# A spectral-filter and feed-forward block on one core: first-layer weights in four quarters, twelve tiles transposed by the DMA crossbar, smaller token blocks

## The chip, the cores and the metric

The kernel runs on one core of a Trainium2 chip. The metric is the device time of one execution in microseconds (us). Each comparison was made on one chip in alternating rounds of the changed kernel and the kernel before. An execution's state is *slow* when it is over 1.5% above the fastest of its kernel; comparisons use the others, the *fast* ones. The median given with an experiment is over all its executions, the ratio over the fast ones alone. A profile is one execution.

## The reference

The input x has 2048 tokens of 640 features in bf16. Its layer norm goes two ways: through a two-dimensional FFT, a product with a complex filter and the inverse FFT, and through a feed-forward layer with 1536 hidden units. Both results are added to x.

```python
xn = layernorm(x)                                   # over the 640 features
a  = irfft2(rfft2(xn) * (w_r + 1j * w_i))           # filter of 2048 x 321
b  = gelu(xn @ w1 + b1) @ w2 + b2                   # 640 -> 1536 -> 640
out = x + a + b
```

## The kernel before

The FFTs are matrix products with small tables. The stages, by the names that the profile shows: `gtab` (first FFT step, along tokens), `etab` (along features), `mtab` (second token step, out of the copy `Xb`), the filter product on DVE (`T<-Y,Wf`), `ntab`, `getab` and `htab` (the inverse). Among these stand the matmuls of the first layer, `xnT,W`, and of the second, `W,gT`. They are TensorE's filler: whenever an FFT step waits for a copy, they run.

The profile calls TensorE PE (its weight loads PEld), VectorE DVE, ScalarE ACT, GpSimd POOL and SyncE SP. L12 is line 12 of the kernel.

All operations go to a list scheduler in the kernel itself, which simulates the engines with rough durations and fixes the order on each engine and in the DMA queue by priorities (`PRIO`). PSUM banks are dealt out from zones (`ZONE`). So a changed priority or block size can change the whole order.

Sixteen tiles of 128 tokens are normalized by DVE. The first layer needs them with the features on the partitions, `xnT`. The first eight are transposed on TensorE through PSUM, the others by the crossbar in the DMA:

```python
if c < BYPE:                                   # BYPE = 8
    ...                                        # five transposes on TensorE, then a copy on DVE or ACT
else:
    ring_ops.append(K.op([("sp", 1.25)], 50, lambda e, _, c=c, xnv=xnv: e.dma_start(
        xnT[:, :, 128 * c:128 * c + 128], xnv(0, [[1, D]]), transpose=True), ...))
```

The filter `Wf` is loaded by eight large loads (rows as they lie, pieces of 10,272 bytes) and ten for the mirrored rows. These have to be read in reverse order, so they go in pieces of one row, 642 bytes; the eight longest have 240 or 256 such pieces each. A load may start only after the load four places earlier has landed (`DEPTH = 4`). The first filter product waits for all of them:

```python
for j, row, n in ((0, 128 - m1, 16),) if m1 else ((0, 64, 1), (1, 127, 15)):
    load_w(<rows j..j+n of Wf>, <rows of w_r or w_i, step -321>, ...)      # mirrored
...
K.op([("dve", ...)], pr, <T = Y * Wf>, reads=[Y, B_w, B_wpad], writes=[TB], after=ring_ops)
```

Every one of these loads, and every transpose by DMA, is issued by SyncE into one queue and served by the same 16 DMA engines.

## Time and profile before

| | before |
|---|---|
| median of 3 runs | 159.98 us (158.77 to 160.95) |
| span of the profiled execution | 155.0 us, clock 1.00 |
| TensorE busy | 147.4 us, 95% |
| DVE busy | 124.4 us, 80% |
| transposes by DMA | 8, median 5.8 us from issue to landing |

Three more readings matter for what came. The first is the DMA's busy share in the first 60 us in 40 slices of 1.5 us, one digit each (9 is 90% or more):

```profile
DMA  0769999999999733993799999999999988000000
```

The 16 DMA engines have slack between 19.5 and 30 us (but for two full slices), then work without a gap until 51 us. The second is DVE's timeline at the first filter product (start, length, what):

```profile
51.15 1.57 DVE L713 TENSOR_TENSOR T<-Y,Wf 128x1288 bf16<-128x1288 bf16 x2
```

No bracket follows the line, so DVE did not wait ahead of it: the filter was there. In the DMA's records, the last mirrored piece ended at 47.1 us, and its load was reported as landed at 47.6. The margin was about 3.5 us. The third is the busy time of the engines from 50 to 60 us (PE, PEld, DVE, ACT, POOL, then granted clock, DMA share and GB/s):

```profile
50.00:60.00 10.00, 9.84 (x120) 4.90 (x115) 8.93 (x17) 7.03 (x13) 0.00 (x0) 1.00 0.08 20
```

### The profile page before, as it was taken

The numbers are of one execution on the slowest core, as the hardware profiler recorded it, in microseconds if no ns is written. First come the engines' busy times: TensorE is split into PE (matmuls) and PEld (weight loads), VectorE is DVE, ScalarE is ACT, GpSimd is POOL, SyncE is SP. The second block draws the span as 40 slices with busy tenths as digits, with TensorE's granted clock in tenths as the row PEclk, the third lists the DMA queues.
The fourth block names the chain that finished last, engine by engine and source line by source line (L and its number), as shares of the span: only waits on it lengthen the run. The fifth ranks groups of instructions, "written<-read, shape, count | busy, mean of one in ns | idle before, by whom it ended". The sixth has DMA issues, their size and how long they took to land.

```text
span 155.0 us, 3617 instructions
## 1 busy us (share of the span) xinstructions
PE 147.4 (95%) x1473; PEld 95.5 (62%) x1483; DVE 124.4 (80%) x277; ACT 73.1 (47%) x144; POOL 30.3 (20%) x33
## 2 busy tenths in 40 slices
PE   5699999999999999999999999999999999999993
PEld 2298996545564545454555666777776667777771
DVE  3869999999964989898898797899999989822231
ACT  3077987888776678868767534310101330000000
POOL 1201121110100000000000003009937254444100
PEclk9999999999999999999999999999999999999999
DMA  4999949799999000019141400002533442211111
GB/s 116 346 377 395 329 110 172 98 138 146 101 134 225 18 4 0 4 16 324 25 149 18 156 0 12 34 0 89 169 105 127 123 132 84 73 42 42 63 66 44
DMA packets 18632, 17.85 MB, mean 115 GB/s; under 512 B 6712, under 2 KB 17336, under 8 KB 18488
## 3 DMA queue, kind: packets, MB, share of 16 engines
q1 hardware_dynamic: 18448, 17.59, 47.5%
q8 instruction: 11, 0.18, 0.5%
q10 hardware_dynamic: 168, 0.04, 0.1%
q14 instruction: 5, 0.04, 0.1%
HBM read 13.69 MB, written 2.62 MB: 105 GB/s over the span
## 4 chain that ended last, share of the span: by engine, by line
PE 74%; DVE 14%; DMA 4%; issue 3%; ACT 2%; SPq 1%
PE ps L477 73%; DVE Wf L806 4%; DMA W<-in_B_w_dram 4%; DVE Wf L811 4%; DVE ost L836 3%; DVE Wf L487 2%; ACT gT L657 2%; PE ps L602 1%; DVE xnT L792 1%; SPq L472 1%; ACT xnT L484 0%; ACT b1col L558 0%
## 5 line engine op out<-in xcount | busy, mean ns | idle before, releaser
L477 PE MATMUL ps<-xnT,W 128*128 128x512 bf16 (+2 forms) x350 | 56.6, 306 | 2.7 <-DMA W<-in_B_w_dram 1.3
L477 PE MATMUL ps<-W,gT 128*128 128x320 bf16 x384 | 56.7, 299 | 0.0
L477 PEld LDWEIGHTS ps<-W,gT 128*128 128x128 bf16 x384 | 37.0, 98 | 14.2 <-issue 0.3
L477 PEld LDWEIGHTS ps<-xnT,W 128*128 128x128 bf16 x360 | 28.5, 98 | 19.7 <-issue 1.8
L657 ACT ACTIVATE gT<-ps,b1col 128x512 bf16<-128x512 f32 (+2 forms) x72 | 36.5, 550 | 5.0 <-PE ps L477 4.7
L823 POOL TENSOR_TENSOR xo<-xr,b2bc 128x640 f32<-128x640 bf16 x11 | 16.4, 1494 | 20.9 <-DVE ost L836 20.9
L836 DVE TENSOR_TENSOR ost<-ps,xo 128x640 bf16<-128x640 f32 (+1 forms) x12 | 9.2, 764 | 13.6 <-PE ps L477 13.6
L823 POOL TENSOR_TENSOR xnT<-xr,xnT 128x640 f32<-128x640 bf16 x5 | 7.4, 1490 | 60.3 <-DVE Zs L487 55.0
L484 ACT ACTIVATE Wf<-ps 128x640 bf16<-128x640 f32 x9 | 6.2, 704 | 25.9 <-PE ps L477 25.9
L574 DVE BATCH_NORM_STATS2 stats<-XV 128x6 f32<-128x320 bf16 x32 | 14.3, 474 | 2.3 <-DMA XV<-in_A_x_dram 2.3
L713 DVE TENSOR_TENSOR T<-Y,Wf 128x1288 bf16<-128x1288 bf16 x16 | 12.7, 828 | 0.6
L582 POOL TENSOR_TENSOR rstd<-ve,mhalf 128x2 f32<-128x2 f32 (+1 forms) x9 | 6.2, 693 | 32.1 <-DVE ve L581 32.1
L811 DVE TENSOR_TENSOR Wf<-Wf 128x640 bf16<-128x640 bf16 x16 | 11.8, 775 | 0.1
L806 DVE TENSOR_TENSOR Wf<-Wf 128x640 bf16<-128x640 bf16 x16 | 10.4, 682 | 0.1
L487 DVE CAST Y<-ps 128x644 bf16<-128x644 f32 x8 | 6.6, 828 | 4.4 <-PE ps L477 4.4
L484 ACT ACTIVATE Xb<-ps 128x640 bf16<-128x640 f32 x8 | 7.1, 890 | 4.3 <-PE ps L477 4.3
L477 PE MATMUL ps<-getab,XV 128*128 128x160 bf16 (+1 forms) x128 | 8.6, 233 | 0.4 <-DVE ost L836 0.2
L484 ACT ACTIVATE XW<-ps 128x640 bf16<-128x640 f32 x12 | 8.3, 704 | 1.3 <-PE ps L477 1.1
L484 ACT ACTIVATE XV<-ps 128x640 bf16<-128x640 f32 x9 | 6.2, 703 | 5.6 <-PE ps L477 5.6
L477 PE MATMUL ps<-etab,XW 128*128 128x160 bf16 (+1 forms) x128 | 8.6, 233 | 0.0
L487 DVE CAST Xb<-ps 128x640 bf16<-128x640 f32 x8 | 7.1, 883 | 1.2 <-PE ps L477 1.2
L477 PEld LDWEIGHTS ps<-etab,XW 128*128 128x128 bf16 (+1 forms) x128 | 5.4, 95 | 4.2 <-ACT Xb L484 0.4
(48 smaller groups left out, 140.9 us busy)
## 6 DMA issues: line engine op xcount, KB each, us to landing
W<-in_B_w_dram SPq DMA_DIRECT2D x6, 640.0 KB, 5.5
xr<-in_A_x_dram SPq DMA_DIRECT2D x16, 160.0 KB, 2.3
out_dram<-ost SPq DMA_DIRECT2D x15, 160.0 KB, 1.8
XV<-in_A_x_dram SPq DMA_DIRECT2D x7, 320.0 KB, 9.3
Wf<-in_A_w_r_dram SPq DMA_DIRECT2D x7, 160.5 KB, 10.2
Wf<-in_A_w_i_dram SPq DMA_DIRECT2D x7, 160.5 KB, 5.4
gtab<-c_G SPq DMA_DIRECT2D x1, 512.0 KB, 8.8
htab<-c_H SPq DMA_DIRECT2D x1, 512.0 KB, 3.7
```

What stands on the lines that cost most here:

```text
L472: return K.op([(eng, 0.45)], 0, lambda e, _: e.dma_start(dst, src), reads=reads, writes=[buf], after=after, nbytes=nbytes, rate=rate)
L477: ins = e.matmul(o_, lhsT=lw, rhs=rh, start=st, stop=sp_)
L484: return e.activation(dst(), src(), ACT.Copy, scale=scale)
L487: return e.tensor_copy(dst(), src())
L574: K.op([("dve", 0.4)], 100 - c, lambda e, _, c=c, h=h: e.bn_stats(stats[:, c, 6 * h:6 * h + 6], view(XV, c * D + H2 * h, [[1, H2]])), read ...
L582: K.op([("pool", 0.75)], 100 - c, lambda e, _, a=a, b=b: e.tensor_tensor(out=rstd[:, a:b], in0=ve[:, a:b], in1=mhalf[:, 0:b - a], op=ALU.pow),
L657: K.op([("act", act_us(s1 - s0, 1))], pr + PRIO["gelu"], lambda e, _, s0=s0, s1=s1, fc=fc, hps=hps: e.activation(gT[:, fc, s0:s1], ps(hps. ...
L713: t_ops[pair].append(K.op([("dve", dve_us(4 * KP, 2))], pr, lambda e, _, k=k, Y=Y, TB=TB, pair=pair: e.tensor_tensor(out=view(TT, TB.slot ...
L806: K.op([("dve", dve_us(D, 2))], pr + 2, lambda e, _, k=k, op=op, yo=yo, y2=y2: e.tensor_tensor(out=view(Wf, Y2 + y2.slot * 2 * D + (H2 - 1 ...
L811: K.op([("dve", dve_us(D, 2))], pr + 3, lambda e, _, k=k, op=op, y2=y2, yf=yf: e.tensor_tensor(out=view(Wf, YF + yf.slot * 2 * D + (D - 1) ...
L823: K.op([("pool", pool_us(640))], 50, lambda e, _, c=c, xr=xr, xov=xov: e.tensor_tensor(out=xov(0, D), in0=halves(xrt[:, xr.slot, :]), in1= ...
L836: os_ops.append(K.op([("dve", dve_us(H2 * len(hs)))], 95, lambda e, _, a=a, b=b, hs=hs, xov=xov, fps=fps, os_=os_: e.tensor_tensor(out=hal ...
```

## The change

The change wants TensorE to start earlier and to do less. First-layer weights come in quarters, so that less has to land before the first matmul; twelve tiles instead of eight are transposed by DMA, which takes 20 transposes and four copies off the engines; token blocks are smaller, so that a block can start with fewer tiles. To give the early transposes room, four table loads and one filter load are held back until four transposes have been issued. The other constants (zones, priorities, `AHEAD`, `STAGED`) came with it from a new tuning.

```diff
-ZONE = {'hps': ((0, 8), (4, 8), (4, 8), (0, 4), (6, 8), (6, 8)), 'bps': (0, 6), ...
-PRIO = {'hps': 37.4, ... 'eps': 59.4, 'fin': 18.3, 'fst': 17.7}
-BLOCKS = ((0, 1), (1, 2), (2, 4), (4, 8), (8, 12), (12, 16))
-AHEAD = 3
-STAGED = (0, 2, 4, 7, 9)
+ZONE = {'hps': ((2, 8), (0, 8), (4, 8), (4, 8), (4, 8), (4, 8), (4, 8)), 'bps': (0, 4), ...
+PRIO = {'hps': 61.1, ... 'eps': 12.2, 'fin': 1, 'fst': 14.5}
+BLOCKS = ((0, 1), (1, 2), (2, 4), (4, 6), (6, 9), (9, 12), (12, 16))
+AHEAD = 2
+STAGED = (0, 2, 4, 6, 8)
-BYPE = 8
+BYDMA = (4, 5, 6, 7, 8, 9, 10, 11, 12, 13, 14, 15)
 ...                                                   (durations in the scheduler's model: cut)
-        W1 = sb("W1", [128, 3, 5, 512])
+        W1 = sb("W1", [128, 4, 5, 384])
 ...
         load_w1(0)
         load_w1(1)
+        load_w1(2)
         load_x(2, 2)
-        load_w1(2)
+        load_w1(3)
 ...
-        load(etab[:], ...)  load(mtab ...)  load(ntab ...)  load(getab[:], ...)
+        later = [load(etab[:], ...), load(mtab ...), load(ntab ...), load(getab[:], ...)]
 ...
-            if c < BYPE:
+            if c not in BYDMA:
 ...
+        for o in later + few[0:1]:
+            o.gate += [p for p in ring_ops if p.nbytes][:max(0, len(BYDMA) - 8)]
```

(`W2` is loaded in quarters too. Each list of loads is cut to one line here.)

More of the change, by code (lines that the diff above doesn't have):

```diff
@@ L112, in pool_us @@
     return 0.075 + n / 500.0
-ZONE = {'hps': ((0, 8), (4, 8), (4, 8), (0, 4), (6, 8), (6, 8)), 'bps': (0, 6), 'cps': (0, 6), 'dps': (0, 6), 'eps': (0, 4), 'fps': (2, 8), 'fst': (0, 8), 'yps': (0, 4), 'tps': (0, 2), 'aps': (2, 6)}
-PRIO = {'hps': 37.4, 'gelu': 82.7, 'pb': 120.8, 'pc': 154.1, 'filt': 90.5, 'ipc': 148.4, 'xb': 65.5, 'eps': 59.4, 'fin': 18.3, 'fst': 17.7}
-BLOCKS = ((0, 1), (1, 2), (2, 4), (4, 8), (8, 12), (12, 16))
-AHEAD = 3
-STAGED = (0, 2, 4, 7, 9)
+ZONE = {'hps': ((2, 8), (0, 8), (4, 8), (4, 8), (4, 8), (4, 8), (4, 8)), 'bps': (0, 4), 'cps': (0, 8), 'dps': (0, 4), 'eps': (0, 4), 'fps': (4, 8), 'fst': (4, 8), 'yps': (0, 8), 'tps': (0, 4), 'aps': (0, 6)}
+PRIO = {'hps': 61.1, 'gelu': 149.5, 'pb': 91.9, 'pc': 99.5, 'filt': 154.7, 'ipc': 263.2, 'xb': 214.9, 'eps': 12.2, 'fin': 1, 'fst': 14.5}
+BLOCKS = ((0, 1), (1, 2), (2, 4), (4, 6), (6, 9), (9, 12), (12, 16))
+AHEAD = 2
+STAGED = (0, 2, 4, 6, 8)
 XRAT = 4
@@ L180 @@
 BIAS = {"dve": 0.0}
+FAST = 7
 LAT = {"pe": 0.2, "dve": 0.12, "act": 0.15, "pool": 0.1}
@@ L211, in schedule @@
     def schedule(self):
-        free = {e: 0.0 for e in self.engines}
+        free = {e: 0.75 for e in self.engines}
         dma_free = port_free = 0.0
@@ L281, in schedule @@
             if o.nbytes:
-                s = max(t + 1.3, dma_free)
+                s = max(t + 1.2, dma_free)
                 dma_free = s + o.nbytes / o.rate
-                o.end = dma_free + 1.7
+                o.end = dma_free + (1.8 if o.seq > FAST else 0.6)
             else:
@@ L499, in bass_parallel_sum__spectral_gfnet__dense_activation_gelu__prompt_kernel @@
         B_x = [Buf(f"x{c}") for c in range(16)]
-        B_w1s = [Buf(f"w1_{j}") for j in range(3)]
+        B_w1s = [Buf(f"w1_{j}") for j in range(4)]
         B_g, B_e, B_m, B_n, B_ge, B_h = [Buf(x) for x in "gemnih"]
@@ L509, in load_w1 @@
         def load_w1(j):
-            load(W1[:, j, :, :], w1v[:, :, 512 * j:512 * j + 512], B_w1s[j], 655360)
+            load(W1[:, j, :, :], w1v[:, :, 384 * j:384 * j + 384], B_w1s[j], 491520, rate=340e3)
         load_x(0, 1)
@@ L522, in bass_parallel_sum__spectral_gfnet__dense_activation_gelu__prompt_kernel @@
             load_x(a, 2)
-        load(etab[:], const["E"], B_e, 204800)
-        load(mtab[:].rearrange("p a b c d -> p (a b c d)"), const["M"], B_m, 131072)
-        load(ntab[:].rearrange("p a b c -> p (a b c)"), const["N"], B_n, 98304)
-        load(getab[:], const["GE"], B_ge, 204800)
         few = []
+        later = [load(etab[:], const["E"], B_e, 204800), load(mtab[:].rearrange("p a b c d -> p (a b c d)"), const["M"], B_m, 131072),
+                 load(ntab[:].rearrange("p a b c -> p (a b c)"), const["N"], B_n, 98304), load(getab[:], const["GE"], B_ge, 204800)]
         def load_w(dst, src, nbytes, rate):
@@ L653, in bass_parallel_sum__spectral_gfnet__dense_activation_gelu__prompt_kernel @@
                     part = [K.op([("pe", len(js) * mm_us(s1 - s0))], pr + 0.01 * len(part), mms(lambda s0=s0, s1=s1, fc=fc, hps=hps, js=js: [
-                        (ps(hps.slot, 0, s1 - s0), W1[:, fc // 4, j, 128 * (fc % 4):128 * (fc % 4) + 128], xnT[:, j, s0:s1], j == 0, j == 4) for j in js]),
-                        reads=[B_w1s[fc // 4]] + B_xnT[c0:c1], writes=[hps], gate=part)]
+                        (ps(hps.slot, 0, s1 - s0), W1[:, fc // 3, j, 128 * (fc % 3):128 * (fc % 3) + 128], xnT[:, j, s0:s1], j == 0, j == 4) for j in js]),
+                        reads=[B_w1s[fc // 3]] + B_xnT[c0:c1], writes=[hps], gate=part)]
                 hps_ops.setdefault(blk, []).append(part[0])
@@ L677, in two @@
             return PS[buf.slot // 2][:, :].rearrange("p (b n) -> p b n", b=2)[:, :, 0:2 * Q4].rearrange("p b (n k) -> p n b k", n=2)
-        IPC = 24 * 0.028 + 0.2
-        FIVE = 8 * mm_us(Q4) + 2 * 0.1 + 0.19
+        IPC = 0.78
+        FIVE = 1.0
         pb_ops, filt_ops, cps_ops, t_ops = [], [], {}, {}
@@ L692, in bass_parallel_sum__spectral_gfnet__dense_activation_gelu__prompt_kernel @@
             cps = [Buf(f"cps{pair}_{r}", psum, 2, ZONE["cps"]) for r in range(2)]
-            cps_ops[pair] = [K.op([("pe", 4 * mm_us(KP) + 0.36)], PRIO["pc"] - pair / 5, mms(lambda pair=pair, cps=cps, xb=xb: [
+            cps_ops[pair] = [K.op([("pe", 0.78)], PRIO["pc"] - pair / 5, mms(lambda pair=pair, cps=cps, xb=xb: [
                 (ps(cps[r].slot + hi, 0, KP)[64 * qq:64 * qq + 64], mtab[64 * hi:64 * hi + 64, 1 if pair == qq == 0 else 0, v, r, :],
@@ L712, in bass_parallel_sum__spectral_gfnet__dense_activation_gelu__prompt_kernel @@
             for k in range(2):
-                t_ops[pair].append(K.op([("dve", dve_us(4 * KP, 2))], pr, lambda e, _, k=k, Y=Y, TB=TB, pair=pair: e.tensor_tensor(
+                t_ops[pair].append(K.op([("dve", 0.05 + dve_us(4 * KP, 2))], pr, lambda e, _, k=k, Y=Y, TB=TB, pair=pair: e.tensor_tensor(
                     out=view(TT, TB.slot * 8 * KP + k * 4 * KP, [[2 * KP, 2], [KP, 2], [1, KP]]), in0=yv(Y, k == 1), in1=wv(pair, k), op=ALU.mult),
@@ L761, in bass_parallel_sum__spectral_gfnet__dense_activation_gelu__prompt_kernel @@
                      reads=[dps[hi]], writes=[B_v[2 * pair + hi]], after=norm_ops)
-        B_w2s = [Buf(f"w2_{i}") for i in range(3)]
-        for i in range(3):
-            load(W2[:, 4 * i:4 * i + 4, :], w2v[:, 4 * i:4 * i + 4, :], B_w2s[i], 655360, after=[o for blk in hps_ops for o in hps_ops[blk][4 * i:4 * i + 4]])
+        B_w2s = [Buf(f"w2_{i}") for i in range(4)]
+        for i in range(4):
+            load(W2[:, 3 * i:3 * i + 3, :], w2v[:, 3 * i:3 * i + 3, :], B_w2s[i], 491520, after=[o for blk in hps_ops for o in hps_ops[blk][3 * i:3 * i + 3]])
         all_hps = [o for blk in hps_ops for o in hps_ops[blk]]
@@ L783, in second @@
                     for fc in range(f0, f0 + 2) for h in hs]),
-                    reads=[B_w2s[f0 // 4]] + [B_gT[block_of[c], fc] for fc in range(f0, f0 + 2)], writes=[fps], gate=part)]
+                    reads=B_w2s[f0 // 3:(f0 + 1) // 3 + 1] + [B_gT[block_of[c], fc] for fc in range(f0, f0 + 2)], writes=[fps], gate=part)]
             return part
```

## The prediction

> **What bounds the kernel now.** I first read the busy shares and the slices on the page. The columns of the first line are busy time, share of the span and instructions; the second has one digit per fortieth of the span (3.9 us).
>
> ```profile
> span 155.0 us, 3617 instructions
> ...
> PE 147.4 (95%) x1473; PEld 95.5 (62%) x1483; DVE 124.4 (80%) x277; ACT 73.1 (47%) x144; POOL 30.3 (20%) x33
> ...
> PE   5699999999999999999999999999999999999993
> ...
> PEclk9999999999999999999999999999999999999999
> ```
>
> TensorE is busy at full clock in every slice but the first two and the last. So the time can change only through the work on TensorE, its idle time at the start, the tail after its last matmul, and waits that the new order brings in. Next I read the chain that ended last, in order of time (start, length, what), for the start:
>
> ```profile
> 1.66 5.81 DMA W<-in_B_w_dram
> 7.46 0.14 issue
> 7.60 0.72 PE ps L477 x10
> ```
>
> The first useful matmul waits for the first third of the first-layer weights. Everything before 7.60 us is warm-up and the transpose of tile 0. From there the chain is TensorE almost throughout; DVE takes 14% of it between 97 and 122 us, but TensorE's own timeline has only two waits there (0.24 and 0.18 us), so the two are balanced there. The last matmul ends near 152.4 us; 2.6 us of evacuation and store follow and don't change.
>
> Third, TensorE's groups by shape (count, busy us, mean ns), to see what the change touches:
>
> ```profile
> L477 PE MATMUL ps<-xnT,W 128*128 128x512 bf16 x170 | 41.4, 380 | 1.1 <-issue 0.8
> L477 PE MATMUL ps<-xnT,W 128*128 128x128 bf16 x120 | 8.2, 219 | 1.7 <-DMA W<-in_B_w_dram 1.3 <-ACT gT L657 0.4
> L477 PE MATMUL ps<-xnT,W 128*128 128x256 bf16 x60 | 7.2, 273 | 0.0
> ...
> L602 PE MATMUL ps<-ident,T 128*128 128x128 bf16 x40 | 3.2, 219 | 0.1
> ```
>
> The means are latencies of pipelined matmuls, so I take the pace from the timeline: the distance from one run's start to the next one's, over its count.
>
> ```profile
> 19.72 1.80 PE L477 MATMUL ps<-xnT,W 128*128 128x256 bf16 x15
> 21.36 0.72 PE L477 MATMUL ps<-gtab,T 128*128 128x128 bf16 x10
> ...
> 33.40 3.22 PE L477 MATMUL ps<-xnT,W 128*128 128x512 bf16 x14
> 36.45 0.72 PE L477 MATMUL ps<-gtab,T 128*128 128x128 bf16 x10
> ```
>
> (21.36-19.72)/15 = 0.109 us at 256 columns, (36.45-33.40)/14 = 0.218 us at 512. The ten gtab matmuls run from 21.36 to 21.92, so 0.056 us at 128 columns. Pace is nearly proportional to columns.
>
> Fourth, the side that has to deliver the tiles: the DMA transposes, and DVE before them.
>
> ```profile
> xnT<-T SPq DMA_TRANSPOSE x8, 5.8
> ```
> ```profile
> 12.89 0.49 DVE L574 BATCH_NORM_STATS2 stats<-XV 128x6 f32<-128x320 bf16 x1 [0.21 <-DMA XV<-in_A_x_dram]
> 13.37 0.80 DVE L593 TENSOR_SCALAR T<-XV,mv,rstd 128x640 bf16<-128x640 bf16 x2
> ...
> 18.33 0.80 DVE L593 TENSOR_SCALAR T<-XV,mv,rstd 128x640 bf16<-128x640 bf16 x2
> ```
>
> The first line is the page's list of issues: eight transposes, 5.8 us in the median from issue to landing. Asked one by one, the first two (issued at 28.6 and 30.0 us) took 4.5 and 4.2 us, later ones up to 8.1; the issue alone holds the queue 1.2 to 1.3 us each. The other lines are DVE's timeline: tiles 2 and 3 are normalized at 13.4 us, tiles 4 and 5 at 18.3. DVE has no further gap until 45.2 us.
>
> **What the Trainium skill says.** "TensorE: Matmul & The Clock Gate", section "Wait — 56ns, not 53.3ns?", gives start to start as N / 2.4 GHz + about 2.5 ns when warm; the paces above (56, 109, 218 ns) agree, and I estimate 163 ns for the new width of 384. "VectorE: DVE Perf Modes", "The three transpose paths", lists a 128x128 bf16 transpose at 390 ns on TensorE and 1309 ns by the DMA crossbar; here a transpose occupies TensorE only 56 ns in a stream, and five of them by DMA hold the queue some 1.25 us and land after 4.2 to 8.1 us. So it is relief of TensorE bought with latency. [...]"SBUF — State Buffer", "Who interferes with whom", says that a VectorE operation with two SBUF inputs blocks against a GpSimd operation that reads SBUF; the two L806 operations at 105.1 us took 2.79 us against 0.89 us elsewhere. The change doesn't remove that.
>
> **The change part by part.**
>
> 1. First weights. The thirds landed at 7.46 (1.66 + 5.8) and 9.3 us (2.1 + 7.2): 1.84 us for 640 KB. A quarter is 480 KB in shorter rows, three quarters of that time if the rate holds, so 1.4, or 1.5 if short rows cost something (my allowance). The first quarter lands 0.35 to 0.45 us sooner, near 7.1. A quarter feeds 30 matmuls of 128 columns over two tiles, 30 x 0.056 = 1.7 us, so later quarters, 1.5 us apart, keep ahead. Gain 0.4 us at the start. But three quarters now go ahead of tiles 2 and 3: 4.2 to 4.5 us against 3.7 for two thirds, so those tiles land 0.5 to 0.8 us later (10.2 before).
>
> 2. Twenty transposes of tiles 4 to 7 leave TensorE: 20 x 0.056 = 1.1 us off its path. Their four copies (two of 0.70 us on ACT, the others of 0.48 on DVE) leave too; ACT isn't a bound, and DVE gets a little earlier.
>
> 3. Block sizes. First layer before: 120 x 0.056 + 60 x 0.109 + 180 x 0.218 = 52.5 us. After: 120 x 0.056 + 120 x 0.109 + 120 x 0.163 + 60 x 0.218 = 52.4 us. Nothing. ACT pays more per element in small pieces (485 ns for 256 columns, 682 for 512), at most 48% to 60% busy: off the path.
>
> 4. The new waits at the front. The order of the changed kernel has tiles 0 and 1 completely, then the transposes of 2 and 3 with their gtab work, then the block of tiles 2-3, then that of 4-5; the kernel before had matmuls left between transposes, so TensorE had filler while a tile was copied. Now: matmuls from 7.25 us, 125 of them and transposes at 0.056 end near 14.3. Tiles 2-3 land near 11.0, and DVE, with the same statistics in front (six halves, of which two of tile 4, which land near 13.4), has them normalized at 14.6 and 15.0. Their transposes then end near 15.6, the ACT copy (0.70) near 16.4. The block 2-3 with ten gtab matmuls, 60 x 0.109 + 0.56 = 7.1 us, runs to 23.6. Meanwhile DVE needs some 3.9 us more to normalized tiles 4 and 5 (five half statistics at 0.40, one copy 0.41, small ones 0.5, two normalizations 0.36 each): 18.6 and 19.0. Transposes are issued at 18.7 and 20.0 and land, at 4.3 to 4.5 us, at 23.2 and 24.3. So the block 4-5 starts at about 24.4, after waits of 1 us for tile 3 and 0.8 us for tile 5.
>
> 5. From there the remaining TensorE work is the same: the orders differ only in how it is interleaved. The kernel before reached the corresponding point, its first 512-wide matmul, near 24.9 us (ten transposes at 22.14 and 20 matmuls of 0.109 after them). So what remains of the 1.5 us of parts 1 and 2 is 0.5 us.
>
> Sum: 155.0 - 0.5 = 154.5 us of span. In step with the median of 159.98 (which lies about 5 us above the profiled span), 159.5. The later stages were re-arranged too (priorities, PSUM zones), and somebody tuned them, which makes me put the middle 0.5 us lower: 159.0.
>
> **The rivals.** (a) *The transposes land late.* Just ahead of them the queue holds the rest of x (last landing 18.5 us before) and three loads of the filter weights, which landed at 22 to 23 us before. If the crossbar takes the median 5.8 or more, tile 5 lands at 26 to 28, and TensorE stands 2 to 4 us: 161 to 163. For it: the later transposes did take 6 to 8 us. Against: those queued behind 642-byte pieces of the filter weights, while here the large pieces are ahead, and four table loads (640 KB) have been moved behind. (b) *The whole gain arrives.* If tiles 2-3 and 4-5 are in time, 0.4 + 1.1 + the 0.4 us wait for ACT at 12.17 are saved, some 1.9 us: 158. (c) *A later delivery becomes the bound.* Tile 8 lies behind the four tables and a filter load and lands around 32 us, just when the block of tiles 6-8 begins (24.4 + 6.5 + 1.1); the last filter loads move behind the last transposes, about 4 us later than before, close to the first multiplication by them (51.2 us before). Each could cost 0.5 to 2 us. (d) *DVE in the tail.* The reordered tail runs 47 us from the first inverse matmul to the end, against 56 before, with the same DVE work of some 37 us plus the blocking by GpSimd: up to 1 us.
>
> **Range and chances.** Middle 159.0; rival (b) with better later stages gives 156.5, rival (a) or (c) 162. More than 2% faster would need 3.2 us, above everything that parts 1 and 2 hold, so it must come from the re-tuned rest: 0.15. Slower by 2% needs a stall of over 4 us: 0.07.
>
> **What will show it.** The first xnT matmul near 7.2 us; 20 rather than 40 transposes on TensorE (busy near 146.3); a gap before the 256-wide matmuls, and another, released by the DMA of xnT, before the block of tiles 4-5 at 24 to 25 us; the first 384-wide matmul near 32 us; no more than 1.5 us of idle time later. I am wrong if the transposes land in over 6 us, or if TensorE's idle time between 8 and 150 us shrinks below the 2.5 or so of before.

## The result, and the profile after

| | before | after |
|---|---|---|
| median of the fast runs | 158.77 us (3 of 4 runs, 158.37 to 159.98) | 165.04 us (4 of 4 runs, 164.21 to 165.5) |
| span of the profiled execution, clock | 155.0 us, 1.00 | 163.4 us, 0.979 |
| TensorE busy | 147.4 us | 150.1 us |
| first filter product starts | 51.15 us | 57.04 us |

The ratio is 1.037, with a 95% interval from 1.029 to 1.046: slower by 3.7%, outside the predicted range. A ratio here is the mean time of one kernel's fast runs over that of the other's of the same rounds, so it is not quite the ratio of the medians. The fourth run of before, 160.95 us, is over 1.5% above its fastest and left out (with it, its median is 159.38).

TensorE's slices and its clock, 40 slices of 4.1 us:

```profile
PE   6799999999999349999999999999999799999993
...
PEclk9999999999999956999999999999999999999999
```

Before, both rows were full. Now TensorE is busy for only 30% and 40% of the slices from 53 to 61 us, and from 57 to 65 us its clock is down to 0.5 and 0.6. Its timeline there, and DVE's, with the idle time ahead in brackets and what ended it:

```profile
59.46 1.29 PE L478 MATMUL ps<-Xb,mtab 64*64 64x322 bf16 x16 [4.88 <-DVE Xb L488]
```
```profile
57.04 1.57 DVE L717 TENSOR_TENSOR T<-Y,Wf 128x1288 bf16<-128x1288 bf16 x2 [5.52 <-DMA Wf<-in_A_w_i_dram]
```

TensorE waits for a copy of DVE, but DVE itself stood 5.52 us, at the filter product, which is ahead of that copy in its order, and that one waited for a filter load. The chain of waits, in order of time, says the same:

```profile
44.66 5.31 DMA Wf<-in_A_w_r_dram
49.96 0.02 issue
49.98 6.89 DMA Wf<-in_A_w_i_dram
...
57.04 1.57 DVE T L717 x2
58.62 0.80 DVE Xb L488
59.42 0.04 issue
59.46 5.80 PE ps L478 x52
```

The last filter load is issued at 49.98 us and lands 6.89 us later. The windows show what stood still:

```profile
50.00:60.00 10.00, 5.12 (x58) 2.97 (x61) 3.79 (x6) 3.74 (x7) 0.00 (x0) 0.88 0.80 126
60.00:70.00 10.00, 9.79 (x101) 5.25 (x95) 6.17 (x14) 7.49 (x16) 0.00 (x0) 0.78 0.03 6
```

From 50 to 60 us the DMA share is 0.80, not 0.08; TensorE is busy for half the window; and for part of the next one it runs at half clock. And these are the DMA engines in slices of 1.5 us, as shown for before:

```profile
DMA  0769999999994976998999999999999999995049
```

Most of the slack between 19.5 and 30 us is filled, and the work ends 4.5 us later. Counted by piece size in the DMA's records, with busy time as the sum of their durations over 16 engines: 256-byte pieces, almost all of them of transposes (640 per tile), 5260 before and 7820 after, 13.4 and 18.3 us; mirrored filter pieces 2048 in both, 11.3 and 12.9 us, the last one ending at 47.1 and 56.4 us. Such a sum holds waiting too: between 35 and 50 us, 19 to 21 pieces were under way at a time on the 16 engines, before and after. The 640 pieces of one tile sum to 0.73 to 0.85 us where they run fastest (18 ns each in the median) and to 2 us and more elsewhere. So of the 4.9 us between 13.4 and 18.3, some 3 are what four tiles take at the fastest (an estimate from these); the rest is waiting or a slower pace.

To see where the whole difference sits I computed TensorE's *lag*: the time since the first `gtab` matmul, less the time that the matmuls issued since then need at their undisturbed pace (count times pace, summed over TensorE's order; the paces are those of the prediction and others read likewise).

| lag of TensorE, us | before | after |
|---|---|---|
| first `etab` | -0.2 | 0.9 |
| second `Xb,mtab` group (behind the filter product) | 0.3 | 5.9 |
| the one after that | 0.3 | 8.5 |
| first `getab` | 2.1 | 10.2 |
| end | 3.0 | 12.8 |

The spans differ by 8.4 us: 0.4 for a later start of the first `gtab`, -1.8 because less work is left behind it, and 9.8 of lag (12.8 less 3.0). By the stretches of the table (worked out before rounding), 1.0 of the 9.8 arises at the front, 4.7 at the filter wait (5.1 against 0.4), 2.4 right behind it while the clock is low (2.5 against 0.1), nothing from there to the first `getab`, and 1.7 in the tail after it (2.6 against 0.9), where the longest wait is this one:

```profile
127.86 0.72 PE L478 MATMUL ps<-Wf,htab 128*128 128x320 bf16 x4 [1.27 <-DVE Wf L815]
```

The means of the fast runs differ by less (5.9 us), because the profiled execution of before was a lucky one: 157.06 us, under every other run of it up to here.

### The profile page after: what moved, and what is told of

It is laid out like the page before. It is cut to its first block, busy times and chain, and to the rows that moved or that the text cites.

```text
span 163.4 us, 3712 instructions
## 1 busy us (share of the span) xinstructions
PE 150.1 (92%) x1518; PEld 100.5 (62%) x1523; DVE 123.5 (76%) x261; ACT 80.0 (49%) x168; POOL 31.1 (19%) x33
## 3 DMA queue, kind: packets, MB, share of 16 engines
q1 hardware_dynamic: 21808, 18.25, 50.8%
## 4 chain that ended last, share of the span: by engine, by line
PE 30%; DMA 24%; issue 23%; DVE 15%; SPq 4%; POOL 3%; DVEq 0%; POOLq 0%
PE ps L478 30%; DMA Wf<-in_A_w_r_dram 9%; DMA Wf<-in_A_w_i_dram 8%; DMA XV<-in_A_x_dram 5%; DVE stats L575 4%; SPq L473 3%; DMA xr<-in_A_x_dram 3%; POOL xnT L827 2%; DVE Wf L815 2%; DVE T L594 2%; DVE Wf L810 2%; DVE T L630 1%; DVE ost L840 1%; POOL xo L827 1%; DVE T L717 1%
## 5 line engine op out<-in xcount | busy, mean ns | idle before, releaser
L478 PE MATMUL ps<-xnT,W 128*128 128x128 bf16 (+3 forms) x415 | 57.2, 290 | 2.3 <-DMA W<-in_B_w_dram 0.9
L478 PEld LDWEIGHTS ps<-xnT,W 128*128 128x128 bf16 x420 | 34.3, 98 | 18.0 <-issue 2.9
L661 ACT ACTIVATE gT<-ps,b1col 128x128 bf16<-128x128 f32 (+3 forms) x84 | 39.6, 507 | 10.0 <-PE ps L478 8.8
L827 POOL TENSOR_TENSOR xo<-xr,b2bc 128x640 f32<-128x640 bf16 x11 | 17.1, 1563 | 21.1 <-DVE ost L840 21.1
L485 ACT ACTIVATE Wf<-ps 128x640 bf16<-128x640 f32 x10 | 6.8, 703 | 25.9 <-PE ps L478 25.9
L815 DVE TENSOR_TENSOR Wf<-Wf 128x640 bf16<-128x640 bf16 x16 | 13.4, 869 | 0.1
L478 PE MATMUL ps<-Xb,mtab 64*64 64x322 bf16 x128 | 6.5, 324 | 4.9 <-DVE Xb L488 4.9
L810 DVE TENSOR_TENSOR Wf<-Wf 128x640 bf16<-128x640 bf16 x16 | 10.0, 654 | 0.8 <-ACT Wf L485 0.8
L485 ACT ACTIVATE Zs<-Z 128x128 bf16<-128x128 bf16 (+1 forms) x30 | 5.7, 263 | 8.8 <-DVE Z L722 8.8
L485 ACT ACTIVATE XV<-ps 128x640 bf16<-128x640 f32 x11 | 7.4, 703 | 5.4 <-PE ps L478 5.3
```

What stands on the lines that cost most here:

```text
L478: ins = e.matmul(o_, lhsT=lw, rhs=rh, start=st, stop=sp_)
L485: return e.activation(dst(), src(), ACT.Copy, scale=scale)
L661: K.op([("act", act_us(s1 - s0, 1))], pr + PRIO["gelu"], lambda e, _, s0=s0, s1=s1, fc=fc, hps=hps: e.activation(gT[:, fc, s0:s1], ps(hps. ...
L810: K.op([("dve", dve_us(D, 2))], pr + 2, lambda e, _, k=k, op=op, yo=yo, y2=y2: e.tensor_tensor(out=view(Wf, Y2 + y2.slot * 2 * D + (H2 - 1 ...
L815: K.op([("dve", dve_us(D, 2))], pr + 3, lambda e, _, k=k, op=op, y2=y2, yf=yf: e.tensor_tensor(out=view(Wf, YF + yf.slot * 2 * D + (D - 1) ...
L827: K.op([("pool", pool_us(640))], 50, lambda e, _, c=c, xr=xr, xov=xov: e.tensor_tensor(out=xov(0, D), in0=halves(xrt[:, xr.slot, :]), in1= ...
```

## The experiments

Theory 1: the filter loads are late because of the queue; each waits for the landing of the one four places earlier and holds the transposes behind it, and the held-back tables are in the way. Theory 2: the 16 DMA engines are full, and the four extra transposed tiles, 2560 pieces more, push the last filter piece back; the order of waits hardly matters. Beside these: are quarters, blocks or the tail to blame? In a_nochain, a_early, a_halves, a_halves2 and a_bigs the order on the compute engines is the change's own, in a_order that of a_tail. The other variants went through the scheduler again, so more than the edited line moves in them.

### Queue or engines: four kernels, one chip

**a_nochain** takes away the dependence of filter loads on earlier filter loads; the order on all engines and in the queue stays.

```diff
         K.schedule()
+        for o in few:
+            o.deps = [d for d in o.deps if d not in few]
         K.sync()
```

> The changed kernel with the same order on every engine, except that a filter load no longer waits until the load four places before it has landed. Theory 1 (the issuing queue is held up by these waits and by four more transposes, so the last filter load goes out at 50.0 us and lands at 56.9): without the waits it goes out near 44 us, lands at 49 to 51.5, the first filter multiply starts near 51.7 instead of 57.0, the 4.9 us wait of TensorE and the low clock behind it vanish, span near 156, ratio to before 0.98 to 1.00. Rival (the DMA engines are simply full of 642-byte pieces and transposes): earlier issue, but the last landing stays at 55 or later and the time stays above 162.

Measured: 164.93 us, ratio 1.036 (1.027 to 1.045). The last filter load went out at 47.89 us instead of 49.98, and landed no earlier: at 57.30 instead of 56.87. (Theory 1 had put its issue near 44 us, so only a part of the queue's waits is taken away here.) The filter wait on DVE fell from 5.5 to 3.1 us, but only because tile 5 came late in this execution and so did the work ahead of it; the first filter product began at 57.5 us, as in the change:

```profile
57.48 1.57 DVE L717 TENSOR_TENSOR T<-Y,Wf 128x1288 bf16<-128x1288 bf16 x2 [3.13 <-DMA Wf<-in_A_w_i_dram]
```

The time did not move.

**a_early** moves the held-back loads ahead of the first transposes again, compute orders unchanged.

```diff
         K.schedule()
+        sp = K.order["sp"]
+        first = [o for o in ring_ops if o.nbytes][0]
+        moved = later + few[3:4]
+        rest_ = [o for o in sp if o not in moved]
+        i = rest_.index(first)
+        K.order["sp"] = rest_[:i] + moved + rest_[i:]
         K.sync()
```

> The changed kernel with only the queue's order changed: the four tables and the fourth filter load go out before the first transposes, as in the kernel before. Theory 1: the queue is 2 us further at 29 us, but the waits for landings remain, so the last filter load lands 1 to 2 us earlier (55 to 56) and the wait shrinks to 3 to 4 us; against this the transposes of tiles 4 and 5 queue behind 0.8 MB and land at 25 to 26 us, a wait of 1 to 2 us at the block 4-5. Time 162 to 165. If the move of these loads were the whole cause, the wait at 54.6 us would be gone and the time near 158.

Measured: 164.49 us, ratio 1.036 (1.030 to 1.043). Another wait took the place of the filter's:

```profile
27.58 3.89 PE L478 MATMUL ps<-xnT,W 128*128 128x256 bf16 x20 [4.47 <-DMA xnT<-T]
```

The first two transposes, of tiles 4 and 5, now took 7.5 and 8.2 us to land, and DVE's wait for the filter was down to 1.2 us, with the last filter load landing at 57.9 us. Same sum, other place.

**a_eight** is the changed kernel with eight tiles by DMA (which also empties the gate); the scheduler makes a new order.

```diff
-BYDMA = (4, 5, 6, 7, 8, 9, 10, 11, 12, 13, 14, 15)
+BYDMA = (8, 9, 10, 11, 12, 13, 14, 15)
```

> The changed kernel with eight tiles by DMA instead of twelve (so also without the gate), quarters and blocks kept. Theory 1: the last filter load lands at 46 to 48 us as in the kernel before, no wait at the first multiply, TensorE busy 1.1 us more; time 158 to 160, ratio 0.99 to 1.01. Rival (the new blocks, priorities and PSUM zones cost the time in the middle and tail): still 162 or more.

Measured: 160.7 us, ratio 1.012 (1.005 to 1.019); its profile fell into a slow execution. The last mirrored piece ends at 48.5 us and the filter product doesn't wait.

**b_dma12** does the opposite: the kernel before, with twelve tiles by DMA and nothing else.

```diff
-BYPE = 8
+BYPE = 4
```

> The kernel before with twelve tiles by DMA and nothing else (its tables stay ahead of the transposes). Theory 1: the filter loads land at 54 us or later, TensorE waits 2 to 5 us before the second pair of the spectral chain; 1.1 us of transposes saved; time 161 to 164, ratio 1.01 to 1.03. Rival (the blocks and order are at fault): 158 to 159.5, ratio 0.99 to 1.00.

Measured: 164.74 us, ratio 1.036 (1.029 to 1.043). This one number is as slow as the whole change. Its DMA engines in slices of 1.5 us, and its filter product:

```profile
DMA  0759999999999893949999999999999999806894
```
```profile
54.29 1.57 DVE L713 TENSOR_TENSOR T<-Y,Wf 128x1288 bf16<-128x1288 bf16 x2 [1.81 <-DMA Wf<-in_A_w_i_dram]
```

Here the larger part is lost at the front: the lag is 5.4 us at the first `etab` already (waits of 2.19 us for DVE and 0.92 us for a transpose, and low clock after them), 7.5 behind the filter product. DVE had no gap during the 2.19 us, so the scheduler's new order has a share in this loss, and that its total equals the change's is in part chance. What the run shows of the DMA is that with four more tiles, and the tables where they were, the last filter load lands at 54.1 us instead of 47.6. With a_nochain and a_early, theory 1 is out as the main cause.

### Fewer pieces, or less in front of the first product

**a_halves** loads the mirrored rows in halves, all second halves behind all first ones, and lets the first three of the eight filter products wait for first halves only. Pieces and compute orders are those of the change.

```diff
+        for o, one, two_ in mirrored:            # p: copy of the load o
+            o.emit, p.emit, p.deps = one, two_, []      # rows 0..7, rows 8..15
+            extra.append(p)
+        K.order["sp"] = sp[:at] + extra + sp[at:]       # behind the last first half
+        for pair in range(3, 8):
+            for o in t_ops[pair]:
+                o.deps = o.deps + extra
```

> The changed kernel with the same order on all compute engines and the same 642-byte pieces, but the mirrored filter rows of the last five pairs are loaded after those of the first three, and the first three pairs' multiplications wait only for theirs. Theory 2 (after a_nochain: the DMA engines are full without a gap from 18 to 56 us, and the last filter load lands late because of the bytes and pieces in front of it): about 6 us of pieces no longer stand in front, the first filter multiply starts at 51.5 to 53 instead of 57.0, the wait at 54.6 us is under 1.5 us, time 157.5 to 160, ratio 0.99 to 1.005. Theory 1 (the queue's issue is late): the issue times of the first half hardly change, the first multiply stays at 55 or later, time above 162.

Measured: 159.67 us, ratio 1.009 (1.001 to 1.017), over the fast runs. One of its four executions took 249.65 us, at a mean clock of 0.565, and that was the profiled one:

```profile
PE   7999999999999999999999999999999999999995
...
PEclk9555555555555555555555555555555555555555
```

The clock stayed near half for the whole program although TensorE had no pause over 0.4 us. The trace has one granted clock of 0.56 for it, where the others have stretches of 1.0 and 0.5, and its 320-column matmuls followed each other after 228 ns in the median (136 in a_tail), so this is not the fall described below. No other of the executions did so; I have no cause for it and leave it out of all comparisons. The same kernel was therefore run again as **a_halves2**.

> The same kernel as a_halves again, because its profile fell into an execution at half clock. Theory 2: in a fast execution the first filter multiply starts at 51.5 to 53.5, no wait of TensorE at the second Xb group above 1 us, clock 0.99 or more; left over are a wait of about 2 us for the DMA transpose of tile 5 and 2.5 us of waits after the first inverse matmul; time 158 to 160, ratio 1.00 to 1.015.

Measured: 160.07 us, ratio 1.005 (0.995 to 1.015); two of the four executions were slow (163.33 and 161.18 us), two fast (158.96 and 158.67). In the profiled one, a slow one, the filter product didn't wait, but it came only at 56.7 us, because TensorE had waited 3.37 us for tile 5 and then ran at half clock for a slice. In the fast runs the loss of the change is mostly gone. A profile of this edit in a fast execution is that of a_tail below, whose order is the same up to the last stage. There the product ran without a wait:

```profile
52.65 1.57 DVE L724 TENSOR_TENSOR T<-Y,Wf 128x1288 bf16<-128x1288 bf16 x2
```

**a_bigs** (relative error 0.028): it loads the mirrored rows unreversed, in pieces of 10 KB, so that the bytes stay and most of the pieces go. Its output is wrong, which doesn't matter for the time.

```diff
-   dst ap=[[WP, 16], [321, n], [1, 321]]     src ap=[[128 * 321, 16], [-321, n], [1, 321]]
+   dst ap=[[WP, 16], [1, 321 * n]]           src ap=[[128 * 321, 16], [1, 321 * n]]
```

> Wrong on purpose: the changed kernel in which the mirrored filter rows are loaded unmirrored, so 10 KB pieces take the place of 642-byte pieces (same bytes, same number of loads, same places in the queue). Theory 2: 2048 pieces that took 12.9 us of all 16 engines become 128 pieces of about 7 us, the last landing comes 4 to 6 us earlier (51 to 53), first multiply at 51.7 to 53, time 157.5 to 160. If the issue of the twelve transposes were the bound, the landing stays at 55 or later, time above 162.

Measured: 160.29 us, ratio 1.015 (1.008 to 1.023). The last large piece of the filter ends at 50.8 us, and the product runs without a wait, at 52.68 us:

```profile
52.68 1.57 DVE L717 TENSOR_TENSOR T<-Y,Wf 128x1288 bf16<-128x1288 bf16 x2
```

So two independent ways of relieving the filter load, one that puts less in front and one that moves fewer pieces, each take 3.5 to 5 us off (by the ratios). What is left, about 1%, is waits for tile 5 of 2.1 to 2.3 us and the tail.

**a_ten** is a_halves with ten tiles by DMA (`BYDMA` from 6; a new order).

> a_halves with ten tiles by DMA instead of twelve: tiles 4 and 5 go through TensorE again. Theory: the wait of about 2 us for the DMA transpose before the block of tiles 4 and 5, seen in three of the four traces with this order, disappears, 0.57 us of transposes come back: 1 to 1.5 us faster than a_halves2. Rival (the same wait only moves to the tiles 6 and 7 or into DVE): no difference above 0.5 us.

Measured: 162.58 us, ratio 1.025 (1.015 to 1.035), and slower than the same with twelve. A miss: the new order waits 2.39 us for tile 8 in place of tile 5, and its executions scatter from 160.8 to 163.7 us (the last of these is slow).

### Quarters and blocks alone, in the kernel before

**b_quarters**: weights in quarters, three of them ahead of tiles 2 and 3 (the hunks for `W1`, `W2` and `load_w1` above).

> The kernel before with the first-layer weights (and the second-layer ones in the same space) in quarters, three ahead of tiles 2 and 3. From the two traces, the first quarter lands no earlier than the first third did (both 5.8 us after issue) and tiles 2 and 3 land 1 us later. Expected 159 to 161, ratio 1.00 to 1.01; the first matmul within 0.3 us of before. If the prediction's part 1 had been right: 158.5, first matmul 0.4 us earlier.

Measured: 158.22 us, ratio 1.002 (0.995 to 1.009). No gain. In the change's profile there is none at TensorE's start either:

```profile
7.58 0.72 PE L478 MATMUL ps<-xnT,W 128*128 128x128 bf16 x10 [0.93 <-DMA W<-in_B_w_dram]
```

7.58 us, against 7.60 before. But these two executions are the extremes. In the 13 profiled ones with quarters (a_halves at its low clock left out), the first quarter landed at 6.57 to 7.45 us, 7.0 in the mean, and its first matmul started at 6.81 to 7.58, 7.2 in the mean. In the four with thirds, the first third landed at 7.46 to 8.04, 7.7 in the mean, and the matmul started at 7.60 to 8.17, 7.9 in the mean. So by these executions quarters do start TensorE some 0.7 us earlier; that b_quarters (7.41) gained no time by it stays unexplained.

**b_blocks**: blocks of 1, 1, 2, 2, 3, 3, 4 tiles, with a zone each for the additional ones.

```diff
-BLOCKS = ((0, 1), (1, 2), (2, 4), (4, 8), (8, 12), (12, 16))
+BLOCKS = ((0, 1), (1, 2), (2, 4), (4, 6), (6, 9), (9, 12), (12, 16))
```

> The kernel before with token blocks 1, 1, 2, 2, 3, 3, 4 alone. Tensor work in the first layer stays at 52.4 us; ratio 0.99 to 1.01. If the small blocks were a cause of the loss: above 1.015.

Measured: 159.53 us, ratio 1.015 (1.006 to 1.025). Its total lag is 4.4 us against 3.0 before, without one large wait. The zones that I chose and the new order come with it, so whether small blocks as such cost this is open.

### The tail

**a_tail** is a_halves with the three priorities and `AHEAD` of the last stage as before.

```diff
-... 'eps': 12.2, 'fin': 1, 'fst': 14.5}
-AHEAD = 2
+... 'eps': 59.4, 'fin': 18.3, 'fst': 17.7}
+AHEAD = 3
```

> a_halves with the priorities of the last stage (inverse matmuls, final sums) and the depth AHEAD of the kernel before; orders before the last stage unchanged. Theory: the 2.5 us that TensorE falls behind its own work after the first inverse matmul (0.8 us in the kernel before) come from that order, DVE being asked for the results too early: 1 to 2 us faster than a_halves2. Rival (blocking between DVE and GpSimd whatever the order): within 0.5 us of a_halves2.

Measured: 157.63 us (157.17 to 158.93), ratio 0.997 (0.990 to 1.005), all five executions fast. That is level with before.

**a_best** is the same on a_ten.

> Ten tiles by DMA, filter rows in halves, last stage with the priorities of the kernel before: the gains of a_ten and a_tail add up, 155.5 to 157.5, ratio 0.98 to 0.995, the first version faster than both kernels. If one of the two does nothing: 1.00.

Measured: 161.54 us, ratio 1.013 (1.003 to 1.024), with two of its four executions slow; not the best.

Three more runs asked what the tail is worth alone. **a_tailonly**: the change with only these four constants put back.

> The changed kernel with only the three priorities and AHEAD of the last stage put back; the filter loads as in the change, so the wait of about 5 us for them stays. If the tail is a loss of its own, independent of the filter wait, it comes down by 1.2 to 2.4 us from 165.0, to 162.6 to 163.8 (ratio 1.020 to 1.030), with the filter wait unchanged. Rival: the tail is only disturbed by what the filter wait leaves behind; then putting it back does nothing, 165 us (1.037).

Measured: 164.24 us, ratio 1.041 (1.035 to 1.047), while the change itself had 1.037 (1.029 to 1.046) in its own rounds: no gain to be seen. TensorE's wait behind the filter was 4.91 us (4.88 in the change).

**b_latetail**: the kernel before with the change's four constants.

> The kernel before with only the three priorities and AHEAD of the last stage taken from the change. If they are a loss in themselves: 1.2 to 2.4 us slower, 160.3 to 161 (ratio 1.008 to 1.015), with the lag of TensorE after the first getab matmul up from 0.8 to 2 us or more. Rival: they are only wrong for the new interleaving, or neutral: ratio within 0.5% of 1.

Measured: 159.18 us, ratio 1.007 (1.001 to 1.013); the lag after the first `getab` rises from 0.9 to 1.8 us.

**a_eighttail**: a_eight with the old four constants.

> The changed kernel with eight tiles by DMA and the last stage's priorities of before: quarters, small blocks, gate and new zones stay. If the twelve tiles and the tail are the whole loss, this is level with the kernel before: 158.3 us, ratio 0.995 to 1.005. Rival: small blocks cost by themselves (b_blocks was at 1.015); then 160, ratio about 1.01.

Measured: 161.02 us, ratio 1.019 (1.015 to 1.024). It should have been level with before; it isn't better than a_eight.

The lag after the first `getab` makes the size clear. It is 2.6 us with the change's constants and 2.2 with the old ones, in three pairs alike (the change and a_tailonly, a_halves2 and a_tail, a_ten and a_best; 2.3 in a_eighttail), against 0.9 in the kernel before. So these four constants account for 0.4 us of the 1.7 in the changed kernel (in the kernel before they cost 0.9); the other 1.3 belong to what I didn't separate (the zones, `STAGED`, the block sizes). That a_tail beat the two fast runs of a_halves2 by 1.2 us is then probably scatter in the front.

### An attempt to beat both

**a_order** is a_tail with the three filter loads that stand ahead of the first four transposes put right behind them in the queue.

```diff
+        front = [o for o in sp[:first[0]] if o in few]
+        rest_sp = [o for o in sp if o not in front]
+        cut = [i for i, o in enumerate(rest_sp) if o in ring_ops][3] + 1
+        K.order["sp"] = rest_sp[:cut] + front + rest_sp[cut:]
```

> The version with halves and the old tail (157.63 us, ratio 0.997) with the three filter loads that stood ahead of the first four transposes put right behind them in the queue; order on all other engines the same. If those loads are what delays the transposes, tile 5 lands about 1.5 to 2 us sooner, the wait of 2.3 us ahead of the block of tiles 4-5 falls to under 0.8 us, and the time to about 156 (ratio 0.985). Rival: it is the x tiles and tables in flight, or the transposes' own pieces: the wait stays at 2 us or more and the time at 157.6 (0.997).

Measured: 162.38 us, ratio 1.028 (1.022 to 1.033), a clear miss. The wait for tile 5 is gone, as expected, and this one stands in its place, at the block of tiles 6 to 8:

```profile
35.22 5.51 PE L478 MATMUL ps<-xnT,W 128*128 128x384 bf16 x23 [3.86 <-DMA xnT<-T]
```

The large pieces of the three loads now run ahead of the transpose of tile 8, and the longer wait costs clock too. With the DMA engines full, the queue's order only chooses who is late.

### When a wait costs clock as well

Two executions with nearly the same wait, 24 to 26 and 26 to 28 us (the columns are those of the windows above; the clock is the third number from the end). First a_nochain, which waited 2.20 us for tile 5, then a_tail, which waited 2.27 us:

```profile
24.00:26.00 2.00, 0.62 (x4) 0.44 (x5) 1.30 (x6) 0.02 (x1) 0.30 (x1) 0.82 0.75 75
26.00:28.00 2.00, 2.00 (x11) 1.44 (x10) 2.00 (x7) 0.75 (x2) 0.00 (x0) 0.50 1.05 297
```
```profile
24.00:26.00 2.00, 0.82 (x8) 0.74 (x9) 1.23 (x5) 0.06 (x1) 0.03 (x1) 1.00 0.75 86
26.00:28.00 2.00, 2.00 (x26) 1.85 (x24) 2.00 (x8) 1.78 (x5) 0.00 (x0) 1.00 1.32 420
```

After the first, TensorE did 11 matmuls in 2 us, at clock 0.50; after the second, 26 at full clock. The Trainium skill, "TensorE: Matmul & The Clock Gate", section "What's actually happening", says that the clock halves after an idle window of about 3.4 us, that the window runs freely, and that about 3.4 us of work bring it back. The 4.88 us wait of the changed kernel agrees: the clock fell, and the lag grew by 2.5 us (2.4 more than before) while it was low. That waits of 2.2 us fall on either side agrees with the free-running phase, but not with 3.4 us as the least pause.

The traces say more. In each that records them (but a_halves), changes of the granted clock within the run lie a multiple of 3.41 us apart. With windows laid along these changes, first a_nochain's last one before its fall, then the two of a_tail that share the pause:

```profile
21.85:25.27 3.42, 1.32 (x13) 0.94 (x10) 2.87 (x11) 2.17 (x5) 0.69 (x1) 1.00 0.93 117
```
```profile
20.45:23.86 3.41, 2.46 (x28) 2.00 (x25) 3.41 (x13) 3.09 (x7) 0.52 (x1) 1.00 1.18 129
23.86:27.27 3.41, 2.09 (x20) 1.88 (x20) 2.64 (x10) 1.19 (x3) 0.17 (x1) 1.00 0.86 178
```

A window need not be idle throughout: a_nochain's had TensorE busy for 1.32 us. In the profiles here, after 20 us, the clock fell behind every full-clock window with at most 1.32 us of busy time and behind none with 1.42 us or more. So here a pause of 2.2 us cost clock where it fell into one window, and not where it was shared between two.

## Why the prediction was wrong

The prediction was 159.0 us, with a range of 156.3 to 162.0; it was 165.04.

**The step that failed** is the second half of rival (c): "the last filter loads move behind the last transposes, about 4 us later than before, close to the first multiplication by them", and its price, "0.5 to 2 us". The mechanism was named; the size was wrong, and step 5, from which the sum was made, had no term for it. The loads came 9.2 us later, not 4 (last piece 56.4 against 47.1 us), the wait added 4.7 us to TensorE's lag and the low clock 2.4 more. What I left out is that the extra transposes are not only *ahead* of the filter in a queue but are *work* for the same 16 engines: 2560 pieces, some 3 us of all of them at the fastest, and 4.9 us as a sum that holds their waiting. I counted transposes as 1.25 us of queue and a landing latency and never summed up the DMA's time, though the slices showed it full from 30 to 51 us. The 9.2 us can't be divided by such sums, as they overlap. The held-back tables and the large filter pieces, which now run until 36.5 us rather than 28.0, are a likely part beside the transposes; a_early shows that moving those alone gains nothing. And the clock I did not think of: I priced each wait at its own length.

**Step 1, quarters:** 0.4 us predicted at the first matmul. The two profiles compared show 0.0, all profiles together 0.7 (7.2 against 7.9 us), so the step was not wrong; but no time was gained by it (b_quarters). Tiles 2 and 3 landed 1.1 us later in the change's profile (11.3 against 10.2), and 0.4 us later in the mean of the same 13 and 4 executions (0.5 to 0.8 predicted).

**Step 2, twenty transposes off TensorE:** right in count (the profile after has 20) and, by working, 1.1 us; the runs show no gain from it, as a wait came in its place. TensorE's busy time rose to 150.1 us instead of falling to 146.3, in part because matmuls at half clock count as busy for longer (2.5 us by the lag).

**Step 3, blocks, "Nothing":** right for TensorE's work; b_blocks at 1.5% says that the blocks with my zones aren't free, by waits too small to name.

**Step 4, waits at the front:** the block of tiles 2-3 started at 16.54 us (16.4 predicted); in the profiled execution the transposes of tiles 4 and 5 landed 4.0 and 3.2 us after issue and TensorE didn't wait. In three executions with the same compute order up to there (a_nochain, a_bigs, a_tail) they took 5.3 to 6.0 us, and TensorE waited 2.1 to 2.3; in the slow one of a_halves2, 6.5 and 7.0 us and a wait of 3.37: rival (a), within its 2 to 4 us. Two slips in the working: its terms for DVE add up to 3.6 us, not 3.9 (the first transpose was issued at 18.65, predicted 18.7), and the last two transposes of before held the queue 2.3 and 1.9 us, not 1.2 to 1.3. The first 384-wide matmul came at 31.83 us, after 0.26 us of waiting for tile 8 (the first half of rival (c), near 32 us).

**Step 5 and the sum:** the first `etab`, the end of this stretch, lies at 47.76 against 47.33 us. So "what remains of the 1.5 us" was nothing. "In step with the median ... about 5 us above the profiled span" was a mistake too: time and span of one execution differ by 2 to 3 us; the rest was the lucky profile.

**Rival (d), the tail,** up to 1 us: measured 1.7 us of lag.

**The chances:** "slower by 2% needs a stall of over 4 us: 0.07" put too little on this, because the one stall I had named next to a saturated resource was not worked out.

What is shown: without the wait for the filter (a_halves, a_bigs), most of the loss is gone; twelve tiles by DMA alone bring a loss as large, though mostly in another place (b_dma12); the queue's waits aren't the main cause (a_nochain, a_early). What is open: how the 9.2 us divide, 1.3 us of the tail, why b_quarters gained nothing, the scatter of tile 5's landing, and the one execution at 0.56 of the clock. No version was faster than before beyond the noise; a_tail is level with it.

## What to carry to other kernels

Before moving work from an engine to the DMA, add up the DMA engines' own busy time by piece, up to the point at which the last load on the path must have landed: small pieces cost the same engines as the weights behind them. If the engines are full there, reordering the queue only moves the wait; fewer pieces or a first product that needs fewer of them help. Price a wait of TensorE above some 2 us with the low clock after it: here 4.9 us of waiting cost about 7.

## What the Trainium skill lacked or had wrong

- "VectorE: DVE Perf Modes", section "The three transpose paths", and "DMA: Bandwidth & Descriptors", section "Latency and other measured facts", give 1309 ns for a 128x128 transpose and 261 GB/s (350 to 400 if contiguous) for DMA transposes. Here one instruction moved five 128x128 blocks, 164 KB from SBUF to SBUF, as 640 pieces of 256 bytes. At the fastest they went through in 0.6 us (49.79 to 50.39 in the profile after), by estimate some 270 GB/s, near that figure; others took 1.5 us with hardly a piece between (36.32 to 37.85). Neither section says what else such an instruction costs: its issue held the queue for 1.2 to 1.3 us as a rule, and it landed 2.6 us after issue at the least and 8.2 at the most.
- "DMA: Bandwidth & Descriptors", section "Anatomy of one DMA", puts some 2 us of fixed cost on a DMA that GpSimd issues, most of it the confirmation of the write, and doesn't say what holds for one that SyncE issues. Here, by SyncE, it was 1.7 and 2.0 us from the last piece to the landing for the first weights (5.75 to 7.46 before, 5.41 to 7.45 after), 1.2 us for the same load in a_tail, and 0.5 us for the last filter load (47.12 to 47.62, 56.35 to 56.87).
- "TensorE: Matmul & The Clock Gate", section "What's actually happening", gives about 3.4 us of idle time for the fall of the clock. Pauses of 2.20 and 2.51 us lowered it in some executions here, pauses of 2.27 and 2.39 us didn't in others. It gives no share of a window that counts as idle; here 1.32 us of busy time in 3.41 still did, and 1.42 us didn't.
- The same page warns that the clock was seen stuck low for over 50 us (section "Seeing it yourself"), but has no case of a whole execution at such a clock without a pause; one of this kernel's took 249.65 us at 0.565.
